# Block 0 of an S5 + GeGLU layer: tiles 2 and 3 of the first block transposed by DMA in place of TensorE, and the last weight chunk issued from ScalarE's queue

## The chip, the cores and the metric

The kernel runs on one core of one Trainium2 chip. A core has TensorE (matmul, called PE in the profile; its weight loads are called PEld), VectorE (DVE), ScalarE (ACT), GpSimd (POOL) and SyncE (SP), which here only issues DMAs. ScalarE can issue DMAs too; the profile calls the two issue queues SPq and ACTq. The metric is the device time of one execution in microseconds (us). The kernel before takes 178.5 us, the median of 9 runs (178.02 to 178.94).

## The reference

One input x of 2048 rows (time steps) and 512 columns in bf16 is layer-normalised over its columns; the result xn goes through two branches whose outputs are added to x.

```
xn = (x - mean(x)) / sqrt(var(x) + eps)
A: Bu = xn @ B_bar.T             # complex, 512 states, as two real matmuls
   h[t] = Lam_bar * h[t-1] + Bu[t]          # a scan over the 2048 rows
   yA = 2 * real(h @ C.T) + xn * Dskip
B: yB = (gelu(xn @ w_gate) * (xn @ w_up)) @ w_down   # 512 -> 1376 -> 512
out = x + yA + yB
```

## The kernel before

The 2048 rows are four blocks of 512 rows, and a block is four tiles of 128 rows. X holds x, XN the normalised tiles with rows on the partitions. The matmuls contract over the 512 columns, so each tile must also be had transposed, with columns on the partitions: XNT[b] for block b, four chunks k of 128 columns. For blocks 1 to 3 a DMA transpose (`TR`, line 722, issued by SyncE, one for each tile) makes XNT from XN. Branch B (`GU`, the matmuls of line 823) multiplies 128-wide slices of w_gate and w_up with XNT; branch A is `BU` (line 734), a scan on VectorE (`CHAIN`), and `DN` (line 864) adds both branches up in PSUM.

Block 0 is special, because at the start nothing has arrived yet. Its first 896 hidden columns are computed the other way round (`GT_mm`, line 698: the transposed tile is the stationary operand and the weights are the moving one) in four column ranges r: 0 to 192, 192 to 384, 384 to 640 and 640 to 896. One `unit(j, r)` is the gate and the up product of tile j and range r, four matmuls over k with both halves side by side in a PSUM bank, and then its evacuation (`GT_evac`): gelu on ScalarE (line 707) and the product with the up half on VectorE (line 710). The tile that these matmuls read is XC, not XNT: x with only the mean subtracted (`sub`, line 932), turned by four TensorE transposes against the identity (`cent_T`, line 673) and copied out of PSUM by ScalarE (line 680). The scale 1/sqrt(var) comes later and is handed to the gelu and to the product as a scalar for each row. Normalised tiles of block 0 are made afterwards (`norms`, line 643) and transposed by the four DMAs of `TR(0)`, for the last hidden columns (`GU(0, [7..10])`) and for `BU(0)`. Fill matmuls (line 920) and the warm-up matmuls (line 913) multiply zeros.

The order of work. TensorE and SyncE run their work in the order in which the program was written down. On VectorE, ScalarE and GpSimd a small list scheduler in the file (`Sched`) chooses the order from estimated durations and the latest start that each operation can have; `order_behind` pins one operation behind another of the same engine, and `ch(...)` pins a chain of VectorE operations. Each PSUM bank (8 of them) is handed out in turn by `next_bank`, and a bank is written again only once what it held has been read.

The loads, in SyncE's order: tile 0 of x, half of the first w_gate chunk, tile 2, the first w_up chunk, tile 3, then the chunks 1, 2 and 3 of w_gate and w_up in pairs (`FCH`: columns 0 to 384, 384 to 640, 640 to 896, 896 to 1376; chunk 3 is `load_W`, used first by `GU(0, [7..10])`). Behind chunk 3 come `tr_par` (line 522, a transpose of the small parameters), `TR(0)`, the load of block 1 (`ld_x(1)`, line 488), the transposing loads of B (line 533), the load of block 2 and `TR(1)`. ScalarE's queue issues tile 1, the other half of the first w_gate chunk, and three loads of 1 KB (`load_par`, line 518), on which `tr_par` waits.

Layer norm of block 0 on VectorE: `stats` (lines 624 and 625) for a tile, `root` (line 627: an addition on VectorE, then a power, line 631, and a copy of the mean, line 632, on GpSimd), `recip` (line 636) and `norms`. Tiles 0 and 1 share one `root`, tiles 2 and 3 another.

Of the kernel before, what the change touches and what calls it, by code (L numbers as in the profile page):

```python
# [77 lines left out]
class Sched:  # L78
# [95 lines left out]
    def _backward(self, span):  # L174
        ops = self.ops
        left = {op.id: len(op.users) for op in ops}
        late = {op.id: span for op in ops}
        ready = {e: [] for e in ENGINES}
        last = {e: [op for op in ops if op.eng == e] for e in INORDER}
        for op in ops:  # L180
            if left[op.id] == 0 and op.eng not in INORDER:
                ready[op.eng].append(op)
        busy = {e: span for e in ENGINES}
        begin = {}
        n = len(ops)
        while n:
            best = None
            for e in ENGINES:
                if e in INORDER:
                    if not last[e] or left[last[e][-1].id]:  # L190
                        continue
                    op = last[e][-1]
                else:
                    if not ready[e]:
                        continue
                    op = max(ready[e], key=lambda o: (min(busy[e], late[o.id]), o.finish, o.id))
                end = late[op.id] if op.kind == "dma" else min(busy[e], late[op.id])
                if best is None or end > best[0]:
                    best = (end, op)
            end, op = best  # L200
            e = op.eng
            if e in INORDER:
                last[e].pop()
            else:
                ready[e].remove(op)
            begin[op.id] = end - op.dur
            if op.kind == "dma":
                begin[op.id] = min(begin[op.id], busy[e] - op.issue)
                busy[e] = begin[op.id]
            else:  # L210
                busy[e] = begin[op.id]
            n -= 1
            for d in op.deps:
                late[d.id] = min(late[d.id], begin[op.id] - LAT(d, op))
                left[d.id] -= 1
                if left[d.id] == 0 and d.eng not in INORDER:
                    ready[d.eng].append(d)
        return begin

    def _forward(self, prio):  # L220
# [11 lines left out]
        nleft = len(ops)  # L232

        def rdy_time(op):
            return max([d.finish + LAT(d, op) for d in op.deps] + [op.nb])

        while nleft:
            best = None
# [52 lines left out]
    def emit(self):  # L291
# [19 lines left out]
        for e in ENGINES:  # L311
            seen = {}
            prog = []
            for op in order[e]:
                need = {}
                for d in op.deps:
                    if d.kind == "eng" and d.eng == e and (e == "tensor" or d is op.behind):
                        continue
                    key = ("e", d.eng) if d.kind == "eng" else ("d", d.id)
                    if seen.get(key, 0) >= d.val:  # L320
                        continue
                    if key not in need or need[key].val < d.val:
# [50 lines left out]
def build(nc, ins, out):  # L373
    with ExitStack() as es:
# [117 lines left out]
        def ld_w(W, Wc, src, ci, queue="sync", after=()):  # L492
            f0, f1 = FCH[ci]
            return S.dma(lambda e: e.dma_start(W.ap[:, :, f0:f1], src[:, f0:f1].rearrange("(k p) f -> p k f", p=128)),
                         512 * (f1 - f0) * 2, writes=[Wc[ci]], tag="ld_w", queue=queue, after=after)
# [40 lines left out]
        def load_W():  # L536
            ld_w(WG, WGc, ins["B_w_gate"], 3)
            ld_w(WU, WUc, ins["B_w_up"], 3)
# [88 lines left out]
        def root(b, j0, j1):  # L627
            mn, sbq, qb, rq = (cols(t, b, j0, j1) for t in (MN, SBQ, QB, RQ))
            mv = Buf("MV%d_%d_%d" % (b, j0, j1), "sb", MVt[b][j0].lo, MVt[b][j1 - 1].hi, MV[b].ap[:, j0:j1])
            op = V(lambda e: e.tensor_scalar(sbq.ap, mv.ap[:, :, 1], EPS_BF16, None, ALU.add), D_TINY, [mv], [sbq], "sbq")  # L630
            GATE["pow"] = POOL(lambda e: e.tensor_tensor(qb.ap, sbq.ap, HALF.ap[:, 0:j1 - j0], ALU.pow), 1100, [sbq, HALF], [qb], "pow")
            POOL(lambda e: e.tensor_copy(mn.ap, mv.ap[:, :, 0]), 200, [mv], [mn], "mn")
            return op, mn, qb, rq

        def recip(qb, rq):
# [50 lines left out]
        def GT_mm(j, r, bank, us, ks=range(KD)):  # L686
            f0, f1 = FR[r]
            w = f1 - f0
            ci = max(0, r - 1)
            Wc = [(WGc, WUc)[u][ci] for u in us]  # L690
            if ci == 0 and us == [0] and len(ks) == 2:
                Wc = [WG0h[ks[0] // 2]]
            dst = PS[bank][:, w * us[0]:w * (us[-1] + 1)].rearrange("p (w f) -> p w f", w=len(us))

            def f(e):
                ins_ = None
                for k in ks:
                    ins_ = e.matmul(dst, XCd(j, k), WGU[:, us[0]:us[-1] + 1, k, f0:f1], start=(k == 0), stop=(k == KD - 1))  # L698
                return ins_
            PE(f, d_pe([w * len(us)] * len(ks)), Wc + XCs[j][ks[0] // 2:ks[-1] // 2 + 1], [BANK[bank]], "GT")  # L700

        def GT_evac(j, r, bank, rs):
            f0, f1 = FR[r]
            w = f1 - f0
            GATE["nh"] = kk = (GATE["nh"] + 1) % 3
            sc, rb = rs
            GATE["last_gelu"] = ACT(lambda e: e.activation(GG[kk].ap[:, 0:w], PS[bank][:, 0:w], ACTF.Gelu_apprx_tanh, scale=sc),  # L707
                                    d_act(w, 1), [BANK[bank], rb], [GG[kk]], "gelu")
            hp = Buf("H0_%d_%d" % (j, r), "sb", H0[j].lo + 2 * f0, H0[j].lo + 2 * f1)
# [9 lines left out]
        def TR(b):  # L719
            tts = list(range(4 * b, 4 * b + 4))  # L720
            for j, tt in enumerate(tts):
                S.dma(lambda e, b=b, j=j, tt=tt: e.dma_start_transpose(
                    XNT[b].ap[:, :, 128 * j:128 * (j + 1)], XN[tt % 8].ap),
                    1.6 * 128 * 1024, reads=[XN[tt % 8]], writes=[XTk[b][j]], tag="tr_x%d" % b, issue=1280.0)
# [206 lines left out]
        def sub(j):  # L931
            return V(lambda e: e.tensor_scalar(XN[j].ap, X[j].ap, MVt[0][j].ap[:, 0:1], None, ALU.subtract),
                     d_dve_ts4x(512), [X[j], MVt[0][j]], [XN[j]], "sub")
        load_par()
        load_W()
        tr_par()
        ACT(lambda e: e.activation(H0[3].ap[:, 0:D], X[1].ap, ACTF.Copy, scale=-1.0 / D, accum_out=NM1.ap), d_act(512) + 90,
            [X[1]], [H0[3], NM1], "mean1")
        ch(*stats(0, 0)); ch(sub(0))
        ch(V(lambda e: e.tensor_scalar(XN[1].ap, X[1].ap, NM1.ap, None, ALU.add), d_dve_ts4x(512), [X[1], NM1], [XN[1]], "sub"))  # L940
        ch(*stats(0, 1))
        op, mn0, qb0, rq0 = root(0, 0, 2)
        ch(op)
        ch(*stats(0, 2)); ch(sub(2))
        ch(recip(qb0, rq0))
# [10 lines left out]
        for j in range(2):  # L956
            ch(norms(0, [j], mn0, rq0, 0))
        ch(*stats(0, 3)); ch(sub(3))
        op, mn2, qb2, rq2 = root(0, 2, 4)
        ch(op)  # L960
        ch(recip(qb2, rq2))
        rss = [(rq.ap[:, i:i + 1], rq) for rq in (rq0, rq2) for i in range(2)]
        def unit(j, r):
            bank = next_bank()
            GT_mm(j, r, bank, [0, 1])
# [109 lines left out]
```

## Time and profile before

| what | value |
|---|---|
| median of 9 runs | 178.5 us (178.02 to 178.94) |
| the profiled execution | 178.13 us, span 176.6 us |
| TensorE busy | 171.9 us, 97% of the span |
| VectorE busy | 162.4 us, 92% |
| ScalarE busy | 90.2 us, 51% |
| GpSimd busy | 9.8 us, 6% |
| granted TensorE clock | 1.000 over the whole span |
| DMA, mean over the span | 81 GB/s; 330, 318, 162, 201 and 236 GB/s in the second to sixth of 40 slices |

The span runs from the first to the last instruction; the time of an execution is 1.53 us longer (178.13 against 176.6). Times inside the span are counted from its start. "Idle before" is the time in which an engine had nothing to do, with what released it; a DMA's "landing" is the time from the start of its issue to the moment its data is there. The page's chain of work that ended last is 95% TensorE, 2% DMA and 1% issue.

### The profile page before, as it was taken

To read this page: it belongs to the slowest core of one execution; us is meant where nothing else is said; L and a number is where in the kernel's file an instruction comes from. 1 tells how busy PE (TensorE), PEld (TensorE's weight loads), DVE (VectorE), ACT (ScalarE), POOL (GpSimd) and SP (SyncE) were. 2 spreads that over 40 slices of the span, in tenths; PEclk is the share of its full clock that TensorE was granted. 3 is DMA by queue.
4 is the path that set the end of the run, shared out by engine and by line. 5 is a ranking of instruction groups with operands and counts; after the bars stand their busy time and mean duration, and the time that the engine had idled before them with its cause. 6 is when DMAs were issued, how large, how long until landed. Compare 5 with 4: busy or idle time off the path is not lost.

```text
span 176.6 us, 2494 instructions
## 1 busy us (share of the span) xinstructions
PE 171.9 (97%) x873; PEld 83.9 (48%) x888; DVE 162.4 (92%) x283; ACT 90.2 (51%) x169; POOL 9.8 (6%) x25
## 2 busy tenths in 40 slices
PE   7999999999999999999999999999999999999994
PEld 3754464444544444444644444444454444444453
DVE  6888999977999999889999999999999999999961
ACT  4575668899866898003676792000767780000000
POOL 3212030220000000020000000000000000000000
PEclk9999999999999999999999999999999999999999
DMA  5996996975996000011024000002001000000131
GB/s 154 330 318 162 201 236 116 156 114 103 227 308 150 4 0 2 0 59 59 4 58 90 2 0 0 4 9 81 30 10 20 4 0 0 0 0 0 66 134 43
DMA packets 33396, 14.36 MB, mean 81 GB/s; under 512 B 23688, under 2 KB 33384, under 8 KB 33384
## 3 DMA queue, kind: packets, MB, share of 16 engines
q1 hardware_dynamic: 32944, 13.87, 34.4%
q10 hardware_dynamic: 440, 0.33, 0.6%
q8 instruction: 7, 0.11, 0.3%
q14 instruction: 5, 0.04, 0.1%
HBM read 6.46 MB, written 2.10 MB: 48 GB/s over the span
## 4 chain that ended last, share of the span: by engine, by line
PE 95%; DMA 2%; issue 1%; ACT 0%; DVE 0%
PE PS L864 37%; PE PS L823 32%; PE PS L734 16%; PE PS L698 7%; PE PS L797 3%; DMA arena<-in_B_w_gate_dram 2%; ACT L480 0%; PE PS L673 0%; DVE arena L882 0%; PE PS L920 0%
## 5 line engine op out<-in xcount | busy, mean ns | idle before, releaser
L864 PE MATMUL PS<-arena 128*128 128x512 bf16 (+3 forms) x317 | 65.9, 366 | 0.3
L823 PE MATMUL PS<-arena 128*128 128x512 bf16 x258 | 57.5, 379 | 0.3
L864 PEld LDWEIGHTS PS<-arena 128*128 128x128 bf16 (+1 forms) x323 | 30.8, 98 | 35.2
L823 PEld LDWEIGHTS PS<-arena 128*128 128x128 bf16 x264 | 25.8, 98 | 30.4
L767 DVE TENSOR_TENSOR_SCAN arena<-arena 128x512 bf16<-128x512 f32 x32 | 38.8, 1252 | 0.0
L838 ACT ACTIVATE arena<-PS 128x512 bf16<-128x512 f32 x33 | 19.8, 599 | 36.9 <-PE PS L823 33.3
L734 PE MATMUL PS<-arena 128*128 128x512 bf16 x125 | 27.8, 379 | 0.2
L842 ACT ACTIVATE arena<-PS 128x512 bf16<-128x512 f32 x33 | 19.7, 597 | 4.8 <-PE PS L823 4.6
L856 ACT ACTIVATE PS<-arena 128x512 f32<-128x512 bf16 (+2 forms) x17 | 9.6, 581 | 20.4 <-PE PS L864 19.7
L734 PEld LDWEIGHTS PS<-arena 128*128 128x128 bf16 x128 | 12.5, 98 | 14.9
L738 ACT ACTIVATE arena<-PS 128x512 bf16<-128x512 f32 x32 | 17.7, 595 | 2.3 <-PE PS L734 2.3
L882 DVE TENSOR_TENSOR arena<-PS,arena 128x512 bf16<-128x512 f32 (+2 forms) x17 | 10.8, 651 | 5.1 <-PE PS L864 4.5
L844 DVE TENSOR_TENSOR arena<-arena 128x512 bf16<-128x512 bf16 x33 | 13.0, 415 | 1.7 <-ACT arena L842 1.6
L698 PE MATMUL PS<-arena 128*128 128x192 bf16 (+2 forms) x80 | 13.0, 316 | 0.4 <-ACT arena L680 0.3
L624 DVE BATCH_NORM_STATS2 arena<-arena 128x6 f32<-128x512 bf16 x16 | 10.3, 682 | 0.7 <-DMA arena<-in_A_x_dram 0.7
L754 DVE TENSOR_TENSOR arena<-arena 128x4096 bf16<-128x4096 bf16 (+1 forms) x5 | 9.2, 1858 | 0.5 <-ACT arena L619 0.5
L756 DVE TENSOR_TENSOR arena<-arena 128x4096 bf16<-128x4096 bf16 (+1 forms) x5 | 9.2, 1858 | 0.5 <-ACT arena L620 0.5
L698 PEld LDWEIGHTS PS<-arena 128*128 128x128 bf16 x80 | 7.1, 98 | 5.3 <-DMA arena<-in_B_w_gate_dram 0.7
L707 ACT ACTIVATE arena<-PS,arena 128x192 bf16<-128x192 f32 (+1 forms) x16 | 6.7, 448 | 5.3 <-PE PS L698 2.4
L779 DVE TENSOR_TENSOR arena<-arena 128x4096 bf16<-128x4096 bf16 x4 | 9.2, 2288 | 0.1
L780 DVE TENSOR_TENSOR arena<-arena 128x4096 bf16<-128x4096 bf16 x4 | 9.1, 2282 | 0.0
L710 DVE SCALAR_TENSOR_TENSOR arena<-PS,arena 128x192 bf16<-128x192 f32 (+1 forms) x16 | 6.6, 444 | 0.6 <-ACT arena L707 0.5
(84 smaller groups left out, 108.7 us busy)
## 6 DMA issues: line engine op xcount, KB each, us to landing
out_dram<-arena SPq DMA_DIRECT2D x15, 128.0 KB, 1.7
arena<-in_A_x_dram SPq DMA_DIRECT2D x3, 512.0 KB, 4.9
arena<-in_B_w_down_dram SPq DMA_DIRECT2D x1, 1280.0 KB, 7.5
arena<-in_B_w_gate_dram SPq DMA_DIRECT2D x2, 256.0 KB, 5.1
arena<-in_B_w_up_dram SPq DMA_DIRECT2D x2, 256.0 KB, 5.3
arena<-in_B_w_gate_dram SPq DMA_DIRECT2D x1, 480.0 KB, 5.8
arena<-in_B_w_up_dram SPq DMA_DIRECT2D x1, 480.0 KB, 5.9
arena<-arena SPq DMA_TRANSPOSE x25, 2.5
```

The lines of the kernel that those rows point to most:

```text
L624: return (V(lambda e: e.bn_stats(ST[tt].ap, X[tt].ap), d_dve_1x(512), [X[tt]], [ST[tt]], "bnst"), V(lambda e: e.bn_aggr(MVt[b][j].ap, ST[t ...
L698: ins_ = e.matmul(dst, XCd(j, k), WGU[:, us[0]:us[-1] + 1, k, f0:f1], start=(k == 0), stop=(k == KD - 1))
L734: ins_ = e.matmul(PS[bank][:, :], BBT[c][dk].ap[:, 128 * s:128 * (s + 1)], XNT[b].ap[:, dk, :], start=(dk == 0), stop=(dk == KD - 1))
L738: GATE["evBu"] = ACT(lambda e, bank=bank, k3=k3, s=s, c=c: e.activation(SSc[k3][s][c].ap, PS[bank][:, :], ACTF.Copy), d_act(512), [BANK[ba ...
L767: V(lambda e, g=g, rb=rb, init=init: e.tensor_tensor_scan(g.ap, rb, g.ap, init, ALU.mult, ALU.add), d_dve_scan(512), [g, PA[RRr]] + ([CARc ...
L823: ins_ = e.matmul(PS[bank][0:m, c0:c1], W.ap[:, dk, 128 * ft:128 * ft + m], XNT[b].ap[:, dk, c0:c1], start=(dk == 0), stop=(dk == KD - 1))
L838: GATE["last_gelu"] = ACT(lambda e, bg=bg, kk=kk, m=m: e.activation(GG[kk].ap[0:m, :], PS[bg][0:m, :], ACTF.Gelu_apprx_tanh), d_act(512), ...
L842: ACT(lambda e, bu=bu, kk=kk, m=m: e.activation(UPB[kk].ap[0:m, :], PS[bu][0:m, :], ACTF.Copy), d_act(512), [BANK[bu]], [UPB[kk]], "evU")
L844: V(lambda e, kk=kk, m=m, ft=ft, k2=k2: e.tensor_tensor(HTt[k2][ft].ap[0:m, :], GG[kk].ap[0:m, :], UPB[kk].ap[0:m, :], ALU.mult), d_dve_tt ...
L856: ACT(lambda e: e.activation(PS[bank][:, c0:c1], X[tt].ap[:, c0:c1], ACTF.Copy), d_act(c1 - c0), [X[tt]], [BANK[bank]], "seed")
L864: ins_ = e.matmul(PS[bank][:, c0:c1], l_[:, 128 * j:128 * (j + 1)], r_[:, c0:c1], start=False, stop=last and n == len(ops) - 1, skip_group ...
L882: V(lambda e: e.tensor_tensor(OUTB[ko].ap[:, c0:c1], PS[bank][:, c0:c1], XD[tt].ap[:, c0:c1], ALU.add), d_dve_1x(c1 - c0), [BANK[bank], XD ...
```

## The change

Block 0 is prepared in another way.

- Tiles 2 and 3 of block 0 are no longer turned by TensorE. Their `sub` and `cent_T` go away. Each gets its own `root`, `recip` and `norms` at once, and the matmuls of its units read XNT[0], which the DMA transposes of `TR(0)` fill. So the scale is already in the data, and `GT_evac` for them has no scalar operand.
- `TR(0)` is issued in the order tile 2, tile 3, tile 0, tile 1, and the transposes of tiles 2 and 3 are now waited for by `unit(2, ...)` and `unit(3, ...)`.
- Weight chunk 3 leaves SyncE's queue: its two DMAs are issued by ScalarE, behind the gelu of tile 1, range 1, and the gelu of tile 0, range 2 is pinned behind them. On SyncE `tr_par` and the transposes now stand directly behind chunk 2.
- TensorE's order in block 0 becomes: tiles 0 and 1 in ranges 0 and 1 as before; tiles 0 and 1 in ranges 2 and 3, with the gate and the up half as separate matmuls (first the gate of both tiles, then the up of both); then all four ranges of tile 2, then all four of tile 3.
- In the scheduler, a DMA pinned behind another DMA of its queue counts from that one's issue and needs no semaphore wait, and the power's estimate falls from 1100 to 700 ns; the copy of the mean is pinned behind the power.

```diff
         def rdy_time(op):
-            return max([d.finish + LAT(d, op) for d in op.deps] + [op.nb])
+            return max([d.start + d.issue if d is op.behind and d.kind == "dma" else d.finish + LAT(d, op) for d in op.deps] + [op.nb])
...
-                    if d.kind == "eng" and d.eng == e and (e == "tensor" or d is op.behind):
+                    if d.eng == e and (d is op.behind or d.kind == "eng" and e == "tensor"):
                         continue
...
-            GATE["pow"] = POOL(lambda e: e.tensor_tensor(qb.ap, sbq.ap, HALF.ap[:, 0:j1 - j0], ALU.pow), 1100, [sbq, HALF], [qb], "pow")
-            POOL(lambda e: e.tensor_copy(mn.ap, mv.ap[:, :, 0]), 200, [mv], [mn], "mn")
+            GATE["pow"] = POOL(lambda e: e.tensor_tensor(qb.ap, sbq.ap, HALF.ap[:, 0:j1 - j0], ALU.pow), 700, [sbq, HALF], [qb], "pow")
+            S.order_behind(POOL(lambda e: e.tensor_copy(mn.ap, mv.ap[:, :, 0]), 200, [mv], [mn], "mn"), GATE["pow"])
...
-                    ins_ = e.matmul(dst, XCd(j, k), WGU[:, us[0]:us[-1] + 1, k, f0:f1], start=(k == 0), stop=(k == KD - 1))
+                    lhs = XCd(j, k) if j < 2 else XNT[0].ap[:, k, 128 * j:128 * (j + 1)]
+                    ins_ = e.matmul(dst, lhs, WGU[:, us[0]:us[-1] + 1, k, f0:f1], start=(k == 0), stop=(k == KD - 1))
...
-        load_W()
-        tr_par()
         ACT(lambda e: e.activation(H0[3].ap[:, 0:D], X[1].ap, ACTF.Copy, scale=-1.0 / D, accum_out=NM1.ap), d_act(512) + 90,
             [X[1]], [H0[3], NM1], "mean1")
+        tr_par()
...
-        ch(*stats(0, 2)); ch(sub(2))
+        ch(*stats(0, 2))
+        op, mn2, qb2, rq2 = root(0, 2, 3)
+        ch(op)
         ch(recip(qb0, rq0))
+        ch(*stats(0, 3))
+        ch(recip(qb2, rq2)); ch(norms(0, [2], mn2, rq2, 2))
+        op, mn3, qb3, rq3 = root(0, 3, 4)
+        ch(op)
+        TR(0, [2])
 
         fill(2)
         cent_T(0, tb, "AA")
         cent_T(1, [wb])
+        ch(norms(0, [0], mn0, rq0, 0))
+        recip(qb3, rq3); norms(0, [3], mn3, rq3, 3)
+        TR(0, [3, 0])
+        norms(0, [1], mn0, rq0, 1 - 1)
+        TR(0, [1])
...
                 GT_evac(j, r, ub[j, r], rss[j])
-                if j == 0 and r == 0:
-                    cent_T(2, tb)
-        unit(2, 0); unit(2, 1)
-        cent_T(3, [ub[0, 0]])
-        unit(0, 2)
-        unit(1, 2)
-        unit(3, 0); unit(3, 1)
-        unit(2, 2); unit(3, 2)
-        norms(0, [2, 3], mn2, rq2, 2)
-        TR(0)
+        w3 = GATE["last_gelu"]
+        for W, Wc, nm in ((WG, WGc, "B_w_gate"), (WU, WUc, "B_w_up")):
+            w3 = S.order_behind(ld_w(W, Wc, ins[nm], 3, "scalar"), w3)
+        for r in (2, 3):
+            bs = [next_bank(), next_bank()]
+            for j in range(2):
+                GT_mm(j, r, bs[j], [0])
+            for j in range(2):
+                GT_mm(j, r, bs[j], [1])
+                GT_evac(j, r, bs[j], rss[j])
+                if w3:
+                    S.order_behind(GATE["last_gelu"], w3)
+                    w3 = None
+        for j in (2, 3):
+            for r in range(4):
+                unit(j, r)
         ld_x(1)
-        for j in range(4):
-            unit(j, 3)
```

More of the change, by code (lines that the diff above doesn't have):

```diff
@@ L213, in _backward @@
             for d in op.deps:
-                late[d.id] = min(late[d.id], begin[op.id] - LAT(d, op))
+                late[d.id] = min(late[d.id], begin[op.id] + d.dur - d.issue if d is op.behind and d.kind == "dma" else begin[op.id] - LAT(d, op))
                 left[d.id] -= 1
@@ L534, in load_T @@
                       1.4 * 512 * 1024, writes=[b_], tag="tr_" + nm, issue=3000.0)
-        def load_W():
-            ld_w(WG, WGc, ins["B_w_gate"], 3)
-            ld_w(WU, WUc, ins["B_w_up"], 3)
         def load_B():
@@ L697, in f @@
                 for k in ks:
-                    ins_ = e.matmul(dst, XCd(j, k), WGU[:, us[0]:us[-1] + 1, k, f0:f1], start=(k == 0), stop=(k == KD - 1))
+                    lhs = XCd(j, k) if j < 2 else XNT[0].ap[:, k, 128 * j:128 * (j + 1)]
+                    ins_ = e.matmul(dst, lhs, WGU[:, us[0]:us[-1] + 1, k, f0:f1], start=(k == 0), stop=(k == KD - 1))
                 return ins_
-            PE(f, d_pe([w * len(us)] * len(ks)), Wc + XCs[j][ks[0] // 2:ks[-1] // 2 + 1], [BANK[bank]], "GT")
+            PE(f, d_pe([w * len(us)] * len(ks)), Wc + (XCs[j][ks[0] // 2:ks[-1] // 2 + 1] if j < 2 else [XTk[0][j]]), [BANK[bank]], "GT")
         def GT_evac(j, r, bank, rs):
@@ L705, in GT_evac @@
             GATE["nh"] = kk = (GATE["nh"] + 1) % 3
+            hp = Buf("H0_%d_%d" % (j, r), "sb", H0[j].lo + 2 * f0, H0[j].lo + 2 * f1)
+            if rs is None:
+                GATE["last_gelu"] = ACT(lambda e: e.activation(GG[kk].ap[:, 0:w], PS[bank][:, 0:w], ACTF.Gelu_apprx_tanh),
+                                        d_act(w), [BANK[bank]], [GG[kk]], "gelu")
+                V(lambda e: e.tensor_tensor(H0[j].ap[:, f0:f1], PS[bank][:, w:2 * w], GG[kk].ap[:, 0:w], ALU.mult),
+                  d_dve_1x(w), [BANK[bank], GG[kk]], [hp], "hmul")
+                return
             sc, rb = rs
@@ L708, in GT_evac @@
                                     d_act(w, 1), [BANK[bank], rb], [GG[kk]], "gelu")
-            hp = Buf("H0_%d_%d" % (j, r), "sb", H0[j].lo + 2 * f0, H0[j].lo + 2 * f1)
             V(lambda e: e.scalar_tensor_tensor(H0[j].ap[:, f0:f1], PS[bank][:, w:2 * w], sc, GG[kk].ap[:, 0:w], ALU.mult, ALU.mult),
@@ L717, in H0_T, with TR @@
                       3.5 * 224 * 1024, reads=[H0[j]], writes=wr, tag="tr_h0", issue=2100.0)
-        def TR(b):
-            tts = list(range(4 * b, 4 * b + 4))
-            for j, tt in enumerate(tts):
+        def TR(b, js=range(4)):
+            for j in js:
+                tt = 4 * b + j
                 S.dma(lambda e, b=b, j=j, tt=tt: e.dma_start_transpose(
@@ L955, in build @@
         fill(4)
[L956 to L962, printed above, removed]
+        rss = [(rq0.ap[:, i:i + 1], rq0) for i in range(2)] + [None, None]
         def unit(j, r):
```

## The prediction

> **What bounds the kernel now.** I read the chain of waits first, in order of time, since it says which stage can give anything. Its columns are start, length, and what it was.
>
> ```profile
> 1.43 4.27 DMA arena<-in_B_w_gate_dram
> ...
> 5.75 0.50 PE PS L698 x4
> 6.25 0.22 PE PS L920 x4
> 6.47 0.99 PE PS L698 x12
> 7.46 0.22 PE PS L673 x4
> 7.69 2.32 PE PS L698 x20
> 10.00 0.22 PE PS L673 x4
> 10.23 8.21 PE PS L698 x40
> ```
>
> From 5.75 us, when the second half of the first w_gate chunk has landed, the chain is TensorE alone, up to the last product and store at 174.1. The reader is to see the two rows of L673: the transposes of tiles 2 and 3, 0.22 us each, both on the chain. What TensorE waited for, over the whole span (engine and line, waited for, us):
>
> ```profile
> PE PS L913 <- DVE arena L479: 1.0, 1, 1.0
> PE PS L698 <- ACT arena L680: 0.3, 1, 0.3
> ```
>
> Both are before 5.75 us. So an instruction less on TensorE behind that point is worth its step on the chain, and every new wait there costs in full. Next I read SyncE's queue in order of time (start, us, line), since the change puts it ahead of TensorE:
>
> ```profile
> 5.98 1.26 SPq L494 DMA_DIRECT2D arena<-in_B_w_gate_dram  x1
> 7.29 0.69 SPq L494 DMA_DIRECT2D arena<-in_B_w_up_dram  x1
> 8.11 1.30 SPq L522 DMA_TRANSPOSE arena<-arena  x1
> 9.45 5.17 SPq L722 DMA_TRANSPOSE arena<-arena  x4
> 14.67 0.58 SPq L488 DMA_DIRECT2D arena<-in_A_x_dram  x1
> ```
>
> and the landings, asked issue by issue. The chunk-1 and chunk-2 loads issued at 3.19, 3.67, 4.22 and 4.85 take 4.8, 5.1, 5.4 and 5.6 us: there at 7.99, 8.77, 9.62 and 10.45. Chunk 3 is there at 11.78 and 13.19. The small transpose of L522, 8.11 + 5.4 = 13.51, and the first tile transpose, 9.45 + 4.4 = 13.85, are there only behind chunk 3: on this queue what comes later lands later. The fourth, with nothing ahead of it, takes 2.5 us:
>
> ```profile
> arena<-arena SPq DMA_TRANSPOSE x1, 2.5
> ```
>
> Last, VectorE's layer norm of tiles 2 and 3 in order of time, the cover that is now needed:
>
> ```profile
> 5.70 0.69 DVE L624 BATCH_NORM_STATS2 arena<-arena 128x6 f32<-128x512 bf16 x1 [0.24 <-DMA arena<-in_A_x_dram]
> 6.43 0.18 DVE L625 BATCH_NORM_AGGREGATE arena<-arena 128x2 bf16<-128x6 f32 x1
> 7.76 0.68 DVE L624 BATCH_NORM_STATS2 arena<-arena 128x6 f32<-128x512 bf16 x1
> 8.48 0.18 DVE L625 BATCH_NORM_AGGREGATE arena<-arena 128x2 bf16<-128x6 f32 x1
> 8.70 0.36 DVE L932 TENSOR_SCALAR arena<-arena 128x512 bf16<-128x512 bf16 x1
> ```
>
> **TensorE, part by part.** Removed: two groups of four transposes, 2 x 0.22 = 0.44 us of the chain. Added: tiles 0 and 1 in ranges 2 and 3 become 32 matmuls of 256 columns in place of 16 of 512. Steps on the chain: 192 columns 0.99/12 = 0.0825; 384 columns (2.32 - 0.99)/8 = 0.166; 512 columns (8.21 - 8 x 0.166)/32 = 0.215. For 256 I take 0.0825 + (64/192) x 0.084 = 0.110, or half of the 512 step and 2 ns, 0.109. So 32 x 0.1095 = 3.50 against 16 x 0.215 = 3.44: +0.06 (0 to 0.09). The weight loads (98 ns each) hide already beside the shorter 192-column matmuls. Net -0.38 us.
>
> A rule of the Trainium skill weighs against this step. "VectorE: DVE Perf Modes", in "The three transpose paths", puts a 128x128 transpose at 390 ns on TensorE and 1309 ns by DMA, and advises TensorE where a PSUM destination will do. By its figure eight transposes off TensorE would be worth an estimated 3.1 us; the trace has 0.055 us a step on the chain (0.22/4), so the trace's sum stands at 0.44.
>
> **When TensorE comes to tile 2.** 7.46 is the end of the first 12; 12 more of 192 columns follow: 8.45. Then gate of range 2 from 8.45 (chunk there at 7.99), up from 9.33 (8.77), gate of range 3 from 10.2 (9.62), up from 11.1 (10.45): each at least 0.46 us ahead, no wait. Tile 2 starts at 11.95, tile 3 at 11.95 + 8 x 0.166 + 8 x 0.215 = 15.0, the chunk-3 columns at 18.05 in place of 18.43.
>
> **When tile 2 is there.** Tile 3 of x lands at 2.64 + 4.5 = 7.14, and its stats now stand in VectorE's pinned chain ahead of the normalising of tile 2: 7.16 + 0.72 + 0.22 (stats, by the starts above), + 0.19 (reciprocal, L636 to L643 at 6.92 to 7.11) + 0.36 = 8.65. The power of tile 2 is over by then: the addition ends at 6.8, the power takes 0.71. SyncE: chunk 2 ends at 5.93, then `tr_par`, which waits for the 1 KB loads. No wait of SyncE for these shows at 8.11, so they were there by then; they are issued just behind a load that lands at 5.7, and I take 6.5. `tr_par` to 7.8 (7.3 to 9.4), so the transpose of tile 2 goes out at 8.75 (to 9.45) and lands 2.5 later, 11.25; behind chunk 2 as in the row above it would be 10.45 + 0.66 = 11.1. I take 11.3, some 0.65 us ahead of need: no stall. The upper end is the first-transpose row, 4.4: 8.75 + 4.4 = 13.15, a stall of 1.2; the lower end is none, as an early landing gains nothing. If this cover is gone the cost is one for one.
>
> **Tile 3.** Its addition follows at 8.7, power and copy 0.9 more, reciprocal and normalising 0.6: 10.3, or 11.0 with two products (0.37 each) ahead on VectorE. Issue 10.4, landing at 2.5 to 3.5 (the row issued at 24.27, close behind a 512 KB load): 12.9 to 13.9, need 15.0. Cost 0; 0.3 if it takes 4.4 from 11.0 (15.4).
>
> **Chunk 3 on ScalarE.** SyncE loses 1.26 + 0.69 us of issue, ScalarE gains as much, behind the fourth gelu. That needs a product of VectorE (three gelu buffers), so about 9.4. The gelu of tile 0, range 2 waits until some 10.7 to 11.4 instead of 9.8. Behind it stand the other gelus, 0.43 apart; TensorE asks for that bank again at tile 3 (15.0), and ScalarE also loses two 0.6 us copies (L680). No cost. Landing by 9.4 + 1.3 + 5.9 = 16.6 at the outside, need 18.05. But its 960 KB now move beside the transposes, not ahead of them, and no row shows two queues at work with a transpose; I put this into the 4.4 row.
>
> The skill speaks to this: "DMA: Bandwidth & Descriptors", "Queues, rings and completion order", has each DMA engine go round the queues that have work. The rows agree as far as they go: the two halves of the first w_gate chunk, 192 KB each, issued at 1.20 on SyncE and 1.43 on ScalarE, land at 5.1 and 5.7. By that rule a transpose that meets chunk 3 takes perhaps twice its 0.4 us, an estimate from the spacing of landings in this trace.
>
> **VectorE, GpSimd, SyncE behind.** VectorE: two `sub` less (0.7 us), one addition and one reciprocal more (0.33). GpSimd: one power and one copy more (0.9 us) on an engine that is 6% busy. SyncE's transposes of tiles 2, 3, 0, 1 take 1.28 each: 8.75 to 10.0, 10.4 to 14.2, so block 1 of x is issued at 14.25 in place of 14.67. That matters, since the next thin cover is there: the last transpose of block 1 lands at 28.12 + 3.2 = 31.3, and TensorE comes to `BU(1)` at 24.93 + 32 x 0.215 = 31.8. With TensorE 0.38 earlier the 0.5 us is nearly used unless block 1 comes earlier too; I take both moved alike. Later covers are wider: the last `CT` tile (71.4) is due at 73.6, the last state block (163.6) at 164.9.
>
> **Sum.** -0.38 + 0 + 0: the profiled execution's 178.13 (a span of 176.6 and 1.53 around it, which nothing here touches) would be 177.75. It lies 0.37 under the median, so the forecast is 178.5 - 0.38 = 178.1 us, -0.21%. Differences of 0.2% (0.36 us) are about what a measurement of this kernel can tell.
>
> **Rivals.** (1) *Tile 2 comes late, slower.* Chunk 3 from the other queue holds up the transpose. It decides from a landing of 12.7 (11.95 + 0.38 + 0.36), 3.95 us after issue. At 4.4 the stall is 1.2: +0.8, 179.3 us. For it: the only transposes with much weight traffic about took 3.5 and 4.4. Against it: those stood behind that traffic in one queue, and chunk 3 is issued after tile 2's transpose. (2) *The gain is taken back.* A stall of 0.2 to 0.6 us at tile 2 (landing 12.15 to 12.55), at tile 3, or at `BU(1)` if SyncE's queue slips by 0.4: 178.3 to 178.7, say 178.5. For it: three covers of 0.5 to 2 us in place of none. (3) *The reordering by the scheduler shows downstream*, a late product or a late layer norm of block 1, where VectorE is 92% busy: 178.5 to 179.
>
> **How the numbers follow.** Forecast 0.52; rival 1 0.20; rival 2 0.18; rival 3 0.10. The forecast's -0.38 lies at the bound, so it is split: faster 0.40, same 0.12. Rival 2 gives same 0.13, slower 0.05; rival 3 same 0.04, slower 0.06; rival 1 slower 0.20. So faster 0.40, same 0.29, slower 0.31. Range: the forecast less the spread of medians, 177.7, up to rival 1 at 179.3. The forecast's own range is 177.8 to 178.3.
>
> **What would show it.** Right: two L673 groups gone, no wait of TensorE for a transpose, the first GU matmul near 18.05, `BU(1)` without a gap. Wrong: a wait of PE or PEld of line 698 for `arena<-arena` near 12 or 15 us; a wait of L734 near 31.4; a w_gate or w_up wait near 8.5 to 11.

## The result, and the profile after

| | before | after |
|---|---|---|
| median | 178.52 us (178.02 to 179.01, 32 runs) | 179.66 us (179.22 to 181.97, 10 runs) |
| ratio | | 1.0065, 95% interval 1.0053 to 1.0077 |
| the profiled execution | 178.13 us, span 176.6 | 179.86 us, span 178.0 |
| first matmul of `GU(0)` | 18.49 us | 20.20 us |

The kernel became 1.14 us slower; 178.1 was predicted, and the time is above the range (177.7 to 179.3). Some executions ran at a granted clock of 0.991 in place of 1.000: the 181.97 here, which the ratio leaves out, and among the experiments the 181.61 with chunk 3 back on SyncE and 182.67, 182.92 and 183.17 with block 1 of x ahead of tile 1's transpose. The two profiled executions lie 1.73 us apart, because that of before is 0.39 under its median and that of after 0.20 over it. Nearly all of that, 1.71 us, is there at the first matmul of `GU(0)`, so the place to look is block 0.

What TensorE waited for in after (engine and line, waited for, us, times, longest; L695 is the line of `GT_mm` now):

```profile
PE PS L695 <- DMA arena<-arena: 1.9, 1, 1.9
...
```

The two lines that follow it in this view, 1.0 and 0.2 us, are the two waits of before. The first is new: a wait of 1.9 us for a transfer from on-chip memory to on-chip memory, which here is a tile transpose. The chain of waits of after says which one (start, length, what):

```profile
8.77 0.11 DVE arena L626
8.88 5.00 DMA arena<-arena
...
13.92 6.23 PE PS L695 x32
20.15 0.05 issue
20.20 4.91 PE PS L826 x22
```

Between 8.88 and 13.87 the chain is the transpose of tile 2. TensorE's own order of work shows what it cost:

```profile
6.14 5.88 PE L695 MATMUL PS<-arena 128*128 128x192 bf16 x56
13.92 6.23 PE L695 MATMUL PS<-arena 128*128 128x384 bf16 x32 [1.90 <-DMA arena<-arena]
```

Tiles 0 and 1 are through at 6.14 + 5.88 = 12.02; tile 2 is there at 13.9. The two issue queues at this place, SyncE's lines first (the transposes asked one by one; the second line is tile 2's) and then ScalarE's. The second column is how long the issue itself lasts:

```profile
7.62 1.18 SPq L522 DMA_TRANSPOSE arena<-arena  x1
8.88 1.22 SPq L725 DMA_TRANSPOSE arena<-arena  x1
...
9.35 0.46 ACTq L494 DMA_DIRECT2D arena<-in_B_w_gate_dram  x1
9.83 0.54 ACTq L494 DMA_DIRECT2D arena<-in_B_w_up_dram  x1
```

and the landings of tile 2's transpose and of the two halves of chunk 3, each asked at its issue (KB where given, us from issue to landing):

```profile
arena<-arena SPq DMA_TRANSPOSE x1, 5.0
...
arena<-in_B_w_gate_dram ACTq DMA_DIRECT2D x1, 480.0 KB, 4.4
arena<-in_B_w_up_dram ACTq DMA_DIRECT2D x1, 480.0 KB, 5.3
```

The reader is to see three things. Tile 2's transpose goes out at 8.88, about as early as was forecast (8.75). Chunk 3's w_gate goes out 0.47 us *after* it, on the other queue; since a transpose's issue lasts 1.22 us and this load's 0.46, w_gate's issue lies inside the transpose's and is over first (9.81 against 10.10). And the transpose is reported done at 8.88 + 5.0 = 13.88, just behind w_gate, 9.35 + 4.4 = 13.75, instead of the 2.5 us that it takes alone.

The DMA packets of this execution show what the transpose waited for. Here q1 is SyncE's queue and q10 ScalarE's; each row is packets, MB and the share of 16 engines' time, in three stretches: 10.12 to 11.02, 11.02 to 12.53 and 12.53 to 13.46 us.

```profile
q1 hardware_dynamic: 506, 0.13, 77.2%
q10 hardware_dynamic: 38, 0.04, 28.3%
...
q10 hardware_dynamic: 374, 0.36, 89.3%
...
q10 hardware_dynamic: 272, 0.25, 94.5%
q1 hardware_dynamic: 32, 0.00, 1.9%
```

In the first stretch the 0.13 MB of tile 2 go, and the chunk's first packets beside them. In the second SyncE's queue starts no packet at all; the chunk has the engines to itself. In the third, 32 packets of 0.00 MB in all follow on SyncE's queue, and then the transpose is reported. I read these as its marks of completion. So the data was through 2.1 us after the issue began, and what came late, with the end of the chunk, was the report.

### The profile page after: what moved, and what is told of

Read it like the earlier page. It is cut to its first block, busy times and chain, and to the rows that moved or that the text cites. A ratio compares the mean times of both kernels' runs of the same rounds, so it can differ in the third digit from the quotient of the medians.

```text
span 178.0 us, 2520 instructions
## 1 busy us (share of the span) xinstructions
PE 171.8 (96%) x881; PEld 85.2 (48%) x896; DVE 160.2 (90%) x283; ACT 87.7 (49%) x167; POOL 10.5 (6%) x27
## 4 chain that ended last, share of the span: by engine, by line
PE 91%; DMA 6%; SPq 1%; issue 1%; ACT 1%; DVE 0%; DVEq 0%; ACTq 0%
PE PS L867 37%; PE PS L826 32%; PE PS L737 15%; PE PS L695 4%; PE PS L800 3%; DMA arena<-arena 3%; DMA arena<-in_B_w_up_dram 3%; ACT arena L711 1%; SPq L498 0%; SPq L502 0%; DVE arena L885 0%; DVE arena L626 0%; DVEq L340 0%; ACTq L340 0%
## 5 line engine op out<-in xcount | busy, mean ns | idle before, releaser
L826 PEld LDWEIGHTS PS<-arena 128*128 128x128 bf16 x264 | 25.8, 98 | 30.4
L737 PEld LDWEIGHTS PS<-arena 128*128 128x128 bf16 x128 | 12.5, 98 | 14.9
L695 PE MATMUL PS<-arena 128*128 128x192 bf16 (+3 forms) x96 | 12.9, 290 | 2.1 <-DMA arena<-arena 1.9
L620 DVE BATCH_NORM_STATS2 arena<-arena 128x6 f32<-128x512 bf16 x16 | 10.4, 682 | 1.3 <-DMA arena<-in_A_x_dram 1.3
L695 PEld LDWEIGHTS PS<-arena 128*128 128x128 bf16 x96 | 8.7, 98 | 5.8 <-DMA arena<-arena 2.2
L627 POOL TENSOR_TENSOR arena<-arena 128x2 bf16<-128x2 bf16 (+2 forms) x7 | 5.3, 763 | 60.2 <-DVE arena L626 59.7
L639 DVE TENSOR_SCALAR arena<-arena 128x512 bf16<-128x512 bf16 x16 | 6.1, 408 | 0.3
```

The source lines that it names most:

```text
L620: return (V(lambda e: e.bn_stats(ST[tt].ap, X[tt].ap), d_dve_1x(512), [X[tt]], [ST[tt]], "bnst"), V(lambda e: e.bn_aggr(MVt[b][j].ap, ST[t ...
L695: ins_ = e.matmul(dst, lhs, WGU[:, us[0]:us[-1] + 1, k, f0:f1], start=(k == 0), stop=(k == KD - 1))
L737: ins_ = e.matmul(PS[bank][:, :], BBT[c][dk].ap[:, 128 * s:128 * (s + 1)], XNT[b].ap[:, dk, :], start=(dk == 0), stop=(dk == KD - 1))
L826: ins_ = e.matmul(PS[bank][0:m, c0:c1], W.ap[:, dk, 128 * ft:128 * ft + m], XNT[b].ap[:, dk, c0:c1], start=(dk == 0), stop=(dk == KD - 1))
```

## The experiments

The theory: a transpose that is in flight when a 480 KB chunk starts on the other queue is reported done only when that chunk has landed. The rivals: SyncE's queue is at fault (chunk 2 ahead of the transposes, `tr_par`), moving chunk 3 costs something by itself, or a transpose at this place takes 4 to 5 us anyway.

**Chunk 3 later.** Issued behind the gelu of tile 1, range 2, and nothing else changed.

```diff
-        w3 = GATE["last_gelu"]
-        for W, Wc, nm in ((WG, WGc, "B_w_gate"), (WU, WUc, "B_w_up")):
-            w3 = S.order_behind(ld_w(W, Wc, ins[nm], 3, "scalar"), w3)
+        w3 = None
...
+                if (j, r) == (1, 2):
+                    w3 = issue_w3()        # the three lines taken out above
```

> The changed kernel, with one thing altered: chunk 3 of the weights is issued by ScalarE behind the gelu of tile 1, range 2 (about 11.0 us) in place of tile 1, range 1 (9.35 us). Theory A, that the transpose of tile 2 is held up by the chunk-3 transfers of the other queue: they now start behind it, the transpose lands at 11.3 to 11.5 us instead of 13.87, TensorE's wait of 1.9 us ahead of tile 2 is gone, and the time is 178.1 us (177.8 to 178.4), faster than both kernels. Theory B, that the transpose is late by itself (a late source on VectorE, or a transpose right behind much weight traffic takes 5 us anyway): landing stays near 13.9, time stays near 179.7.

Measured: 179.47 us (178.19 to 180.73) against 178.44, ratio 1.0059 (1.0032 to 1.0085). Tile 2's transpose, issued at 9.19, now has 1.50 us before the chunk starts (10.69), and lands in 2.5 us: SyncE's queue starts its last packet by 11.32, and the chunk its first one after 11.74. What stands ahead of it on SyncE is the same as in after. TensorE no longer waits for it. But tile 3's, issued at 10.82 between the two halves of chunk 3, takes 5.6. TensorE's order of work in this kernel:

```profile
16.49 3.20 PE L695 MATMUL PS<-arena 128*128 128x384 bf16 x16 [1.15 <-DMA arena<-arena]
```

Only 16 matmuls are left behind the wait, so it is tile 3's. The cause is confirmed for tile 2, and the time does not come back: the next thin cover, tile 3's, takes the hit.

**Only chunk 3 moved.** The kernel before, with chunk 3 issued from ScalarE behind the fourth gelu. The first four gelus are also pinned in their order, and the scheduler has the change's rules for pinned DMAs.

```diff
         load_par()
-        load_W()
         tr_par()
...
-        unit(2, 0); unit(2, 1)
+        w3 = GATE["last_gelu"]
+        for W, Wc, nm in ((WG, WGc, "B_w_gate"), (WU, WUc, "B_w_up")):
+            w3 = S.order_behind(ld_w(W, Wc, ins[nm], 3, "scalar"), w3)
+        unit(2, 0)
+        S.order_behind(GATE["last_gelu"], w3)
+        unit(2, 1)
```

> The kernel before, with only chunk 3 moved to ScalarE's queue, behind the same gelu as in the change; all tiles of block 0 still turned by TensorE. Theory A: the transposes of block 0 are needed only at 18.4 us there, so whatever chunk 3 does to them is covered, and the time is that of before, 178.5 us (178.2 to 178.8). If the issues on ScalarE or the later landing of chunk 3 cost something by themselves: a wait of TensorE at 18.4 us and 178.9 us or more.

Measured: 178.40 us against 178.44, ratio 0.9998 (0.9986 to 1.001). The move costs nothing by itself. Its first transpose shows the same hold, though nobody waits for it here: issued at 8.29, 0.39 us ahead of the chunk, there at 13.29; the chunk at 13.08. The two lines, asked at their issues, read as in after: 5.0 us for the transpose, 4.4 for w_gate.

So the hold needs neither the new order of work nor tile 2; it is a matter of what goes out beside the transpose.

**Chunk 3 in pieces.** The same 960 KB at the same place as eight DMAs of 120 KB.

```diff
-        for W, Wc, nm in ((WG, WGc, "B_w_gate"), (WU, WUc, "B_w_up")):
-            w3 = S.order_behind(ld_w(W, Wc, ins[nm], 3, "scalar"), w3)
+        for n, (W, nm, k) in enumerate([(W, nm, k) for W, nm in ((WG, "B_w_gate"), (WU, "B_w_up")) for k in range(KD)]):
+            w3 = S.order_behind(S.dma(lambda e, W=W, nm=nm, k=k: e.dma_start(
+                W.ap[:, k, f0:f1], ins[nm][128 * k:128 * (k + 1), f0:f1]),
+                256 * (f1 - f0), writes=[W3p[n]], tag="ld_w", queue="scalar"), w3)
```

> The changed kernel with each of the two chunk-3 DMAs cut into four of 120 KB (one for each k), issued at the same point of ScalarE's queue; the bytes are the same. Theory A1, that the transpose's completion waits for the one chunk-3 DMA that is under way beside it: it is held for a piece of 120 KB, some 0.4 us, lands at 11.6 to 12.3, the wait of 1.9 us shrinks to 0.3 or less, and the time is 178.1 to 178.5 us. Theory A2, that it waits for the bytes queued on the other queue, in whatever pieces: landing near 13.9 and 179.7 us. Eight issues of about 0.45 us hold ScalarE's gelus until some 13 us, which its buffers should cover.

Measured: 178.88 us (178.46 to 180.07), ratio 1.0036 (1.0018 to 1.0055). Tile 2's transpose, issued at 9.28, lands at 12.38; the first piece, issued 0.40 us after it, lands at 12.18. The hold follows the size of the DMA beside the transpose: 5.0 us with 480 KB, 3.1 with 120 KB. The second piece, issued 0.80 us after the transpose and there at 13.1, did not hold it; it stood behind the first in its queue. More than half of the loss is gone (0.44 us above before in place of 1.14). Part of what remains is another price: the eight issues keep ScalarE's sequencer from 9.68 to 14.6, and TensorE waits 0.3 us for a gelu. ScalarE in order of time, and TensorE's wait:

```profile
9.68 2.08 ACTq L985 DMA_DIRECT2D arena<-in_B_w_gate_dram  x4
11.79 2.75 ACTq L985 DMA_DIRECT2D arena<-in_B_w_up_dram  x4
14.66 1.62 ACT L711 ACTIVATE arena<-PS,arena 128x256 bf16<-128x256 f32 x4 [4.58 <-DVE arena L607]
...
PE PS L695 <- ACT arena L711: 0.3, 1, 0.3
```

**Chunk 3 back on SyncE, ahead of the transposes.** The rest of the change stays.

```diff
         load_par()
+        for W, Wc, nm in ((WG, WGc, "B_w_gate"), (WU, WUc, "B_w_up")):
+            ld_w(W, Wc, ins[nm], 3)
```

> The changed kernel with chunk 3 back on SyncE's queue, directly behind chunk 2 and ahead of the transposes. Theory A in its simple form (a transpose lands behind whatever weights were queued ahead of it): tile 2 lands 0.66 us behind w_up's chunk 3, at 13.2 + 0.7 = 13.9, as in the changed kernel, wait 1.9 us, time 179.7 us: moving chunk 3 to the other queue, at the point where it was put, bought nothing. If two queues at once are worse than one queue in order: faster than the changed kernel by 0.3 us or more. If they are better: slower by 0.3 us or more. SyncE also issues 1.95 us later from there on, so block 1 of x comes later and BU(1) may wait some 0.5 us.

Measured: 180.14 us (179.7 to 181.61, 4 runs) against 178.44, ratio 1.0111 (1.0071 to 1.015). The interval meets that of after (1.0053 to 1.0077), so that this is slower than after is not shown. The transpose of tile 2 goes out at 9.94, behind w_up (7.73, there at 13.63), and lands at 14.24; TensorE waits 1.8 us, against 1.9 in after. Chunk 3 ahead of the transpose in its own queue and chunk 3 issued 0.47 us after it on the other queue cost nearly the same stall.

**Chunk 3 behind tile 3.** As the first experiment, but behind the gelu of tile 1, range 3.

```diff
-                if (j, r) == (1, 2):
+                if (j, r) == (1, 3):
```

> The changed kernel with chunk 3 issued still later, behind the gelu of tile 1, range 3 (about 12.4 us), some 1.6 us behind the issue of tile 3's transpose. Theory A (a transpose issued close to a chunk-3 DMA of the other queue is finished only when that DMA is; one issued 1.5 us ahead of it lands in its own 2.5 us): tile 2 lands near 11.7, tile 3 near 13.4, both ahead of need, and neither wait is left. The transposes of tiles 0 and 1 are held instead, until 17 to 17.6 us, and chunk 3 itself lands at 16.9 and 18; they are due at 18.1 (w_up at 18.9). Time 178.1 us (177.9 to 178.5), faster than before by some 0.3 us. If the cover at 18.1 is too thin: a wait of TensorE at line 826 of up to 0.6 us there and 178.5 to 178.8. If theory A is wrong about tile 3: a wait near 15 as in the run with chunk 3 behind range 2.

Measured: 179.55 us (178.84 to 180.21) against 178.40, ratio 1.0053 (1.0033 to 1.0073). Tiles 2 and 3 go out 3.28 and 1.65 us ahead of the chunk (12.04) and land in 2.5 and 2.4 us. TensorE runs through all units without a stall, and then stands for 2.3 us. Its chain of waits:

```profile
6.38 11.57 PE PS L695 x88
17.96 2.33 issue
20.29 4.91 PE PS L826 x22
```

`GU(0)` reads all four tiles. The transposes of tiles 0 and 1, issued at 11.62 and 13.11, now meet the chunk and land at 16.32 and 20.21 (7.1 us), and chunk 3's w_up itself at 18.09. The stall has moved a second time. The row of 88 matmuls is the best evidence for TensorE's part of the forecast, read below.

**Only tile 2 by DMA.** Tile 3 on TensorE as before, chunk 3 behind the gelu of tile 1, range 2.

```diff
-                    lhs = XCd(j, k) if j < 2 else XNT[0].ap[:, k, 128 * j:128 * (j + 1)]
+                    lhs = XCd(j, k) if j != 2 else XNT[0].ap[:, k, 128 * j:128 * (j + 1)]
...
+        ch(sub(3))
...
+        cent_T(3, [next_bank()])
+        norms(0, [3], mn3, rq3, 3)
+        TR(0, [3])
```

> Half of the change: only tile 2 is turned by DMA, tile 3 by TensorE as in the kernel before; chunk 3 behind the gelu of tile 1, range 2. Theory A: tile 2's transpose is issued 1.5 us ahead of chunk 3 and lands near 11.7, so TensorE waits for no transpose; the other three transposes are held until 16 to 17.7 us, due at 18.3. One group of four TensorE transposes saved, 0.22 us, less the 0.06 us of the split ranges: 178.3 us (178.1 to 178.5). If a transpose beside chunk 3 were late whatever its distance in time: a wait of 1 us or more ahead of tile 2 and 179.3 us.

Measured: 179.10 us (178.03 to 179.72), ratio 1.0032 (1.0014 to 1.0051). Tile 2's transpose, issued 1.49 us ahead of the chunk, lands in 2.5 us. In the profiled execution, 178.45 us, TensorE waits for no transpose; it waits 0.6 us for the first w_up chunk, which is there at 7.45 instead of 6.99 as in after. That execution is 0.65 under the median, so what the others lost is not seen.

**Only tile 3 by DMA.** Chunk 3 stays on SyncE ahead of the transposes, as before; tile 3's transpose goes out second, and its units stand last.

```diff
-                    lhs = XCd(j, k) if j < 2 else XNT[0].ap[:, k, 128 * j:128 * (j + 1)]
+                    lhs = XCd(j, k) if j < 3 else XNT[0].ap[:, k, 128 * j:128 * (j + 1)]
...
+        ld_w(WG, WGc, ins["B_w_gate"], 3)
+        ld_w(WU, WUc, ins["B_w_up"], 3)
...
+        TR(0, [0, 3, 1])
...
+        unit(2, 0); unit(2, 1)
+        norms(0, [2], mn2, rq2, 2)
+        TR(0, [2])
+        unit(0, 2); unit(1, 2)
+        unit(2, 2)
+        for j in range(3):
+            unit(j, 3)
+        for r in range(4):
+            unit(3, r)
```

> A half of the change that leaves the queues as they were before: only tile 3 is turned by DMA, chunk 3 stays on SyncE ahead of the transposes, and tile 3's units come last on TensorE. The transposes go out in the order 0, 3, 1, 2; tile 3's goes out near 10.9 and lands near 14.4 behind chunk 3, due at 15.1. Theory A: no new wait, one group of four transposes saved: 0.22 us, 178.2 us (178.0 to 178.4). If normalising tile 3 early holds SyncE (issue of block 1 of x after 15.1 in place of 14.67): BU(1) waits and the time is 178.4 or more.

Measured: 178.12 us (177.87 to 179.33) against 178.45, ratio 0.9992 (0.9976 to 1.0008). The interval holds 1. A second measurement:

> The kernel with only tile 3 turned by DMA, chunk 3 on SyncE ahead of the transposes and tile 3's units last, measured a second time, since its first interval (0.9976 to 1.0008) holds 1. If one group of four TensorE transposes is worth its 0.22 us of the chain and nothing waits: about 0.2 us below the kernel before, ratio 0.9985 to 0.9990, as in the first measurement (178.12 against 178.45). If the first difference was chance: ratio 1.000 +- 0.001. If a thin cover opens in some executions, as in the other variants: above 1.001, with a wait of TensorE for a transpose in the profile.

Measured: 178.07 us (177.57 to 178.4, 12 runs) against 178.41, ratio 0.9976 (0.9965 to 0.9988). The medians differ by 0.33 and 0.34 us; the second interval leaves out 1, the first does not. So this version is faster than after, and probably by 0.1 to 0.2% than before. `GU(0)` begins at 18.25 and 18.37 in the two profiled executions, against 18.49 in before, which fits the 0.22 us of one group. The chain of waits of the first of the two, in block 0:

```profile
7.48 0.22 PE PS L669 x4
7.70 10.50 PE PS L695 x60
18.20 0.05 issue
18.25 5.13 PE PS L826 x23
```

One group of transposes (L669) is left, and 60 matmuls follow without a gap. Tile 3's transpose stands behind chunk 3 (13.28) and lands at 14.39; its first matmul is 16 steps before 18.20, at about 15.1. The cover is 0.7 us.

**One queue.** All on SyncE: tile 2, w_gate of chunk 3, tile 3, w_up, tiles 0 and 1, block 1 of x. If the other queue is what holds a transpose, this order should be free of it.

```diff
         TR(0, [2])
+        ld_w(WG, WGc, ins["B_w_gate"], 3)
...
-        TR(0, [3, 0])
+        TR(0, [3])
+        ld_w(WU, WUc, ins["B_w_up"], 3)
+        TR(0, [0])
```

> The changed kernel with nothing on the other queue: chunk 3 is issued by SyncE between the transposes, w_gate behind tile 2, w_up behind tile 3, then tiles 0 and 1 and block 1 of x. Theory A (in one queue a transpose lands right behind what is ahead of it, and nothing behind it holds it): tile 2 is issued at 8.8 and lands at 11.3 (due 12.0), tile 3 lands behind w_gate at 13.4 to 14.0 (due 15.0), w_up near 15.8, tiles 0 and 1 near 16.5 (due 18.1): none of TensorE's three waits in block 0 is left. Block 1 of x is issued at 15.1, 0.45 us later than before, so its last transpose is 0.1 to 0.4 us late for BU(1) near 31.4. Time 178.2 to 178.5 us. If it is the mere presence of chunk 3 behind a transpose that holds it, in whatever queue: tile 2 lands near 13.9 as in the changed kernel, 179.7.

Measured: 178.27 us against 178.45, ratio 1.0001 (0.9981 to 1.0022), with eight executions at 177.95 to 178.45 and four at 178.94 to 179.72. The profiled one is of the four (179.19). In it tile 2, issued 1.27 us ahead of w_gate, lands in 2.4 us, but tile 3, issued at 10.73 between the two halves, lands at 16.23 and TensorE waits 1.4 us. The landings of w_gate, tile 3 and w_up, each asked at its issue:

```profile
arena<-in_B_w_gate_dram SPq DMA_DIRECT2D x1, 480.0 KB, 4.1
arena<-arena SPq DMA_TRANSPOSE x1, 5.5
arena<-in_B_w_up_dram SPq DMA_DIRECT2D x1, 480.0 KB, 5.5
```

So one queue did not keep tile 3's transpose on time in this execution.

**One queue, block 1 of x ahead of tile 1's transpose.**

```diff
         norms(0, [1], mn0, rq0, 1 - 1)
+        ld_x(1)
         TR(0, [1])
```

> As the run with one queue, with block 1 of x issued ahead of tile 1's transpose. Theory A: no wait of TensorE in block 0; tile 1's transpose goes out at 14.4, behind 512 KB, and lands at 17.6 to 18.1, due at 18.05, so there is 0 to 0.3 us of wait; block 1 of x comes 0.7 us earlier than before, so BU(1) waits for nothing. Time 178.1 us (177.9 to 178.4).

Measured: 181.9 us (180.27 to 183.17, 6 runs), ratio 1.0173 (1.0125 to 1.0222). Tile 1's transpose, issued at 14.88 behind the 512 KB of block 1, lands at 21.18. In TensorE's waits `GU(0)` stands from 18.4 to 21.6:

```profile
PE PS L826 <- DVE arena L621: 3.2, 1, 3.2
```

The line names VectorE's statistics of block 1, over at 21.4; tile 1 was there 0.2 us before. Either would have stalled `GU(0)`; the trace does not divide the 3.2 us between them.

Tile 3's transpose stands here as in the kernel with one queue: issued at 11.12 between the halves of chunk 3, with w_gate ahead (10.50) and w_up behind (12.38). But it lands in 4.0 us instead of 5.5, near 15.1, 0.6 us behind w_gate:

```profile
arena<-arena SPq DMA_TRANSPOSE x1, 4.0
```

**One chunk between.** The one-queue order with w_up moved behind all four transposes.

```diff
-        ld_w(WU, WUc, ins["B_w_up"], 3)
         TR(0, [0])
         norms(0, [1], mn0, rq0, 1 - 1)
         TR(0, [1])
+        ld_w(WU, WUc, ins["B_w_up"], 3)
```

> All on SyncE: tile 2, w_gate chunk 3, tile 3, tile 0, tile 1, w_up chunk 3, block 1 of x. Only the w_up chunk is moved against the kernel with one queue, where tile 3's transpose, issued at 10.73 us, landed at 16.23, 2.0 us behind the w_gate chunk ahead of it (14.2) and 1.2 us ahead of the w_up chunk behind it (17.47). If the chunk issued behind the transpose holds it: tile 3 is there within 0.7 us of the w_gate chunk, by 14.9, and TensorE has no wait at 15. If it is the chunk ahead alone: tile 3 lands at 16 again, a wait of some 1.2 us. Either way w_up, issued at some 14.6 instead of 12, lands near 19 to 20, and TensorE waits 1 to 2 us for it at 18, so the time is 179 to 180.5 us; the landing of tile 3 is what is read.

Measured, in one run: 178.79 us. w_gate, issued at 10.19, lands at 14.39; tile 3, issued at 10.81, at 15.01, 0.62 behind it instead of 2.0:

```profile
arena<-arena SPq DMA_TRANSPOSE x1, 4.2
```

TensorE has no wait there. The forecast wait for w_up at 18 did not come either (it landed at 18.69 while `GU(0)` had begun at 18.50 with the gate half); instead block 1 of x came at 21.51, and `BU(1)` waited 0.5 us. Taken alone, this would put the 5.5 us of the one-queue kernel down to w_up, issued *behind* the transpose. But with block 1 of x ahead of tile 1, w_up followed tile 3's transpose at the same distance (1.26 us, against 1.24), and the transpose took 4.0. So w_up's place does not decide it. What held tile 3 in that one execution stays open; eight of the twelve executions of the one-queue kernel lack the loss.

Clean cases, a transpose with nothing of chunk 3 ahead of it (us; landings are given to 0.1; in the fifth row both DMAs are in one queue):

| kernel, tile | issued | next chunk issued after it by | chunk there | transpose there | took |
|---|---|---|---|---|---|
| after, 2 | 8.88 | 0.47 (480 KB) | 13.75 | 13.88 | 5.0 |
| only chunk 3 moved, 0 | 8.29 | 0.39 (480 KB) | 13.08 | 13.29 | 5.0 |
| chunk 3 behind tile 3, 0 | 11.62 | 0.42 (480 KB) | 16.14 | 16.32 | 4.7 |
| in pieces, 2 | 9.28 | 0.40 (120 KB) | 12.18 | 12.38 | 3.1 |
| one queue, 2 | 8.83 | 1.27 (480 KB) | 14.2 | 11.23 | 2.4 |
| only tile 2, 2 | 9.36 | 1.49 (480 KB) | 14.95 | 11.86 | 2.5 |
| chunk 3 later, 2 | 9.19 | 1.50 (480 KB) | 14.89 | 11.69 | 2.5 |
| chunk 3 behind tile 3, 3 | 10.39 | 1.65 (480 KB) | 16.14 | 12.79 | 2.4 |

With the chunk 0.5 us or less behind it, the transpose is reported 0.1 to 0.2 us after the chunk; from 1.3 us on it takes its own 2.5, as in three more cases (tile 2 with chunk 3 behind tile 3, and in the last two one-queue kernels, 1.27 to 3.28 us ahead of the chunk). Where between 0.5 and 1.3 us this turns was not tried. The issue of a transpose lasts 1.2 to 1.3 us in all these kernels: in the first four rows the next DMA was issued while it still ran, in the others after it.

The Trainium skill has a rule that fits: "DMA: Bandwidth & Descriptors", "Queues, rings and completion order", says that the increment of a semaphore is a write that lands only after every earlier write of the same DMA engine, whichever queue that came from. The first four rows of the table agree with it, and so do the packets of after: the transpose's data was through by 11.02, and its 32 last packets stood until w_gate's end. Whether they stood by that rule, or because the engines were busy with the chunk, no run here tells apart.

## Why the prediction was wrong, point by point

**TensorE, -0.38: right.** The 88 matmuls without a stall, in the kernel with chunk 3 behind tile 3, took 11.57 us; by the forecast's steps they are 24 x 0.0825 + 32 x 0.1095 + 16 x 0.166 + 16 x 0.215 = 11.58. They start 0.09 earlier than in before (6.38 against 6.47) and end 0.47 earlier (17.96 against 18.43), so the two removed groups less the shorter matmuls are 0.38.

**When TensorE comes to tile 2, 11.95: right.** It was 12.02, with 0.3 us of a weight load's wait for the first w_up chunk on the way, which the forecast had not.

**When tile 2 is issued, 8.75: right, by another way.** The norm of tile 2 ended at 8.85 (8.65 forecast), issue 8.88. `tr_par` was later than thought: SyncE waited 1.4 us for the 1 KB loads and issued it at 7.62; they had been put at 6.5. It did not matter, as the norm came last.

**When tile 2 is there, 11.3, no stall: wrong, and this is the step that failed.** The landing was taken from the transpose that has nothing else in flight (2.5 us), and chunk 3's effect was put into a rival with the 4.4 us row. In place of the 2.5 the trace has 5.0, in place of no stall 1.90. The argument against the rival, that chunk 3 is issued after tile 2's transpose, does not hold: being issued 0.47 us earlier, with the transpose's own issue running for 1.22, protected nothing; 1.3 us did. The estimate by the round of the queues (twice 0.4 us, so 0.4 more) is too small as well: the trace has 2.5 more. And the upper end, 4.4, was not the worst row at hand: the small transpose of L522 stood in the prediction with 5.4, by which the stall would have been 2.2.

**Rival 1: chunk 3 did hold up the transpose; the term was mis-sized.** It had a landing of 4.4 and a stall of 1.2, so +0.8 and 179.3. With the measured terms: -0.38, +0.07 (12.02 for 11.95), +1.90, and +0.13 for the 32 matmuls behind the stall (6.23 for 6.10; 3.20 for 3.05 with the 16 matmuls behind the stall of the first experiment, so it goes with the restart and not with the step). That is +1.72, and the units end at 20.15 against 18.43. The chance of 0.20 was too low: no row of before had a transpose beside a load of another queue, and this unknown was given a price but not a high chance.

**Tile 3, cost 0: right in after, only because of tile 2's stall.** It was issued at 10.51 (10.4 forecast) but landed at 15.71 instead of 12.9 to 13.9, 5.2 us, with w_up issued 0.68 ahead of it. At the forecast due time of 15.0 that is a stall of 0.7; in the experiment that freed tile 2 it was 1.1. Rival 2's thin covers were real: tile 3, then tiles 0 and 1 for `GU(0)`, then `BU(1)` in the last experiment, took the hit in turn. (The recorded 0.3 for a landing at 15.4, due at 15.0, is 0.4; it is in no sum.) Rival 3 did not come: 1.71 of the 1.73 us are there when `GU(0)` begins.

**Chunk 3 on ScalarE.** "No cost" was right for ScalarE's own work: it issued at 9.35 (9.4 forecast), the gelu behind it started at 10.50 (10.7 to 11.4), and both halves were there at 15.13 (16.6 at the outside); the kernel with only this part of the change runs in 178.40. Wrong was to leave the transposes beside it at nothing.

**`BU(1)`: no wait, as forecast, but untested.** Block 1 of x was issued at 14.37 (14.25), there at 18.77 as in before. With TensorE 1.7 us late, the cover was wide.

## What to carry to other kernels

For a DMA whose landing is waited for, look at what any queue issues until its own issue is over, 1.2 us for a tile transpose here: a 480 KB load issued 0.4 to 0.5 us behind a tile transpose doubled its landing, and one issued 1.3 us behind it did nothing. Being first in the order is no cover, and the landing of a lone DMA is no price for one in traffic; price it by its neighbour's landing. And when a step that is worth 0.22 us is paid for by new waits, do only that part of it whose transfer has cover left: one tile, the last one, in place of two gave the 0.1 to 0.2%.

## What the runs showed that was not expected

The data of a transpose can be through long before it is reported: 11.02 and 13.88 in after. Between the two halves of chunk 3 in one queue a transpose took 5.5 us in one kernel and 4.0 in another, and 4.2 with only one half near it. Behind a chunk that is already in flight a transpose took 4.0 to 7.1 us and came 0.6 to 2.1 us after it; why so differently stays open.

The variants with thin covers spread far more than the kernel before (178.02 to 179.01): 178.19 to 180.73 with chunk 3 later, 177.95 to 179.72 with one queue. The landing of the first w_up chunk alone was 6.99 us in after and 7.45 in the kernel with only tile 2 by DMA.
